# Order of weight conversions and of matmul passes in a fused attention and two-MLP kernel

## The chip, the cores and the metric

The kernel runs on one core of a Trainium2 chip. The metric is the device time of one execution in microseconds (us). Three timed runs of the kernel before gave 647.45, 649.16 and 648.88 us; their median is 648.88 us. A further execution was taken with a profile, and all rows below are from that one.

## The reference

Three stages follow one another, on float32 inputs. The first is a causal linear attention with decay on q, k, v of shape (2, 8, 768, 64); its output, transposed, is x with 1536 tokens of 512 values. The second is a gated MLP, the third an MLP with a cosine:

```python
def _moe_ref(x, w_gate, w_val, w_out):          # 512 -> 1536 -> 512
    g = x @ w_gate
    silu = g * (1.0 / (1.0 + np.exp(-g)))
    val = x @ w_val
    return silu * val @ w_out

def _moe2_ref(x, w_in, w_out):                  # 512 -> 2048 -> 512
    h = x @ w_in
    return (h * np.cos(h)) @ w_out
```

In the reference the weights and inputs have 32 or 64 bits: the inputs are cast to float32, the weights arrive as float64 and are read as pairs of 32-bit words.

## The kernel before, in words

*Number format.* TensorE multiplies tiles of type float32r. To keep precision each operand is split into a high part and a low part (wh and wl, xh and xl, gh and gl), and each product is made of three matmul passes, high by low, low by high and high by high, added in one PSUM bank (`mm3`, L101). One matmul takes a 128x128 stationary operand and a 128x512 moving one. A split (`split`, L96) is a copy on ScalarE, which makes the high part, and then a subtraction on VectorE, or on GpSimd for weights, which makes the low part.

*Conversion of a weight piece.* A piece is 128x512 weights. Its raw words (512 KB) come by a DMA from SyncE's queue into one of three `raw` buffers (`load_piece`, L118). ScalarE makes a scaled copy `ct` (`scale`, L134, two buffers). VectorE builds the float32 value `cw` in three steps (`conv_steps`, L172: L180, L182, L186; three buffers). Then, in the program some operations later, `flush` (L212) writes the split: wh on ScalarE (L98) and wl on GpSimd (L99). When a piece's third step is issued, the next DMA is issued. `convert(t, n)` (L228) runs behind each step of the plan: it issues up to n conversion steps, and more if the next step of the plan needs the piece. A piece has a slot in a ring; 13 slots at first (10 and 3), and 7 more (`RING_C`) when the memory of the x sums is free. `held` (L147) stops a conversion whose slot is still in use. The table `PACE` (L35) gives n by the kinds of operations in a step.

*Stages.* Attention runs in 12 chunks (to about 78 us); the first products of the first MLP run in its last chunks. Tokens lie in three blocks of 512. In the first MLP the first two columns (of 128 of the 1536 inner values) are computed the plain way: per block a gate product of 12 matmuls, a val product of 12, then the activation and a down product of 12 (`op_down`, L631). The other ten columns are seven-product columns, in five groups of two: blocks 0 and 1 and gate and val are treated as a 2x2 by 2x2 product with seven products in place of eight, in four operations q1 (four products, 24 matmuls, L567), q2 (L586), q3 (L596) and q4 (L603) of one product each (6 matmuls). They need sums of weights (sa and sb, four additions on GpSimd, `conv_sums`, L192) and sums of x (t1 to t4, `t_sums`, L518), which are made on VectorE and ScalarE in four stages behind the first plain steps; the scratch space of the sums is the result tile of block 2. Block 2 has plain gate and val products in each group, and down products are put between all these. In the second MLP a step has an in2 product (12 matmuls, `op_in2`, L609) and a down product (12) that belongs to an in2 step three steps earlier; a group has four columns and three blocks, so 12 such steps.

*Activation.* `activation` (L495) multiplies on VectorE (L499), copies gh on ScalarE (L500), and puts gl (L502, VectorE) into a list, `low`, that `low_parts` (L672) empties behind the step's conversions.

*Order.* Each engine executes its instructions in the order in which the program issues them (`manual_schedule`); the loop at L742 to L759 therefore sets the order on every engine. Accumulators and products have four PSUM banks each (`acc` and `mm`). At the end of a group the accumulators are copied (L653, ScalarE, or L655, VectorE, in the first group) or added (L657, VectorE) into the block's sum. At the end of the first MLP the sum y is split on ScalarE and GpSimd (L660), four pieces a block.

Of the kernel before, what the change touches and what calls it, by code (L numbers as in the profile page):

```python
# [20 lines left out]
GROUP1 = 2  # L21
GROUP2 = 4
# [10 lines left out]
RAW_AGE = 2  # L33

PACE = {"gate+val": 2, "gate+val+down": 3, "q1": 4, "down": 1, "gate": 3, "in2": 2, "in2+down": 2}  # L35
WARM = 10
# [4 lines left out]
def kernel(  # L41
# [19 lines left out]
    nc = tc.nc  # L61
# [8 lines left out]
    NF1 = FF1 // P  # L70
# [30 lines left out]
    def mm3(ps, w, x, first, last, **kw):  # L101

        (wh, wl), (xh, xl) = w, x
        nc.tensor.matmul(ps, wh, xl, start=first, stop=False, **kw)  # L104
        nc.tensor.matmul(ps, wl, xh, start=False, stop=False, **kw)  # L105
        nc.tensor.matmul(ps, wh, xh, start=False, stop=last, **kw)  # L106

# [36 lines left out]
    grown = [10 ** 6]  # L144
# [486 lines left out]
    def op_down(ph, blk, f):  # L631
# [10 lines left out]
        for i in range(4):  # L642
            ps = acc[ph, gi, blk][i]
            cs = slice(i * P, (i + 1) * P)
            if ph == 0:
                mm3(ps, (hi[:, cs], lo[:, cs]), (gh, gl), first, last)
            else:
                mm3(ps, (gh[:, cs], gl[:, cs]), (hi, lo), first, last)
            if not last:
                continue  # L650
            sm = sums[ph, blk][:, i, :]
            if first_group and ph == 0:
                nc.scalar.activation(sm, ps, AF.Copy)  # L653
            elif first_group:
                nc.vector.tensor_copy(sm, ps)  # L655
            else:
                nc.vector.tensor_tensor(out=sm, in0=ps, in1=sm, op=ALU.add)  # L657
# [14 lines left out]
    def low_parts():  # L672
        while low:
            low.pop(0)()


    with tc.manual_schedule():
# [62 lines left out]
        begun = len(HALVES) // 2  # L740
        convert(begun - 1, 0)
        for t in range(begun, len(steps)):  # L742
            kinds = [op[0] for op in steps[t]]
            n = PACE.get("+".join(kinds), 0)
            if kinds[0] == "q1":
                if t - begun == 3:
                    t_sums(3)
                convert(t - 1, n)
                n = 0
            for nm, *args in steps[t]:  # L750
                run[nm](*args)
            convert(t, n)
            low_parts()
            if t - begun < 3:
                t_sums(t - begun)
            if steps[t][0] == ("q4", NF1 - 1):
                xt_stack.close()
                ring.append(ctx.enter_context(tc.tile_pool(name="ring_c", bufs=RING_C)))
                grown[0] = n_conv[0]  # L759
# [30 lines left out]
```

## Time and profile before

| | before |
|---|---|
| timed runs, us | 647.45, 648.88 (median), 649.16 |
| profiled execution, us | 646.99 |
| its span, first to last instruction, us | 645.2 |
| TensorE matmul (PE), busy us (share), instructions | 614.3 (95%), 3139 |
| TensorE weight load (PEld) | 500.6 (78%), 3141; one load 0.19 us |
| VectorE (DVE) | 475.0 (74%), 709 |
| ScalarE (ACT) | 295.9 (46%), 506; one gh copy (L500) 0.62 us |
| GpSimd (POOL) | 195.3 (30%), 175; one wl (L99) 1.32 us |
| mean granted TensorE clock | 0.989 |
| DMA | 49.3 MB, 76 GB/s over the span |

The profile is of one execution. A busy time is the sum of an engine's instructions; matmuls overlap, so 614.3 us of PE does not mean that the rest, 31 us, is all that could be saved, and starts of matmuls are a better measure than their busy time. A wait is listed with the instruction that waited, and with the one that released it, as far as semaphores tell. The clock is given as a share of full speed: 1.00 is 2.4 GHz and 0.50 is 1.2 GHz.

### The profile page before, as it was taken

How to read it: one execution, taken by the hardware profiler on the slowest of the kernel's cores; microseconds unless marked ns; L12 is line 12 of the kernel's file. 1: busy time of each engine (PE TensorE's matmuls, PEld its weight loads, DVE VectorE, ACT ScalarE, POOL GpSimd, SP SyncE). 2: the span in 40 equal slices, each digit the busy share in tenths (PEclk: the TensorE clock that was granted, in tenths of full speed). 3: DMA queues.
4: the chain of work that ended last, by engine and by line, in shares of the span. 5: the costliest groups of instructions: out<-in, count | busy, mean ns of one | idle time of the engine just before them, and what ended most of it. 6: DMA issues, size and time to landing. Idle time of an engine off the chain costs nothing.

```text
span 645.2 us, 8290 instructions
## 1 busy us (share of the span) xinstructions
PE 614.3 (95%) x3139; PEld 500.6 (78%) x3141; DVE 475.0 (74%) x709; ACT 295.9 (46%) x506; POOL 195.3 (30%) x175
## 2 busy tenths in 40 slices
PE   8999997898999999999999969999999999999997
PEld 5888885686887887887887857888778877887786
DVE  4677578857787777777777895788688777778655
ACT  2353326544334334434435454555555655555442
POOL 3324305726425425525512751011111111111000
PEclk9999999899999999999999998999999999999999
DMA  9997221121211221222222111211211122220103
GB/s 187 204 238 190 67 66 48 54 93 41 92 56 58 84 66 58 74 65 66 66 66 72 60 36 62 65 56 43 70 61 66 65 66 67 65 66 0 67 1 132
DMA packets 65433, 49.32 MB, mean 76 GB/s; under 512 B 38760, under 2 KB 60272, under 8 KB 65392
## 3 DMA queue, kind: packets, MB, share of 16 engines
q1 hardware_dynamic: 65360, 48.77, 26.7%
q8 instruction: 25, 0.41, 0.3%
q14 instruction: 16, 0.13, 0.1%
q10 hardware_dynamic: 32, 0.01, 0.0%
HBM read 45.61 MB, written 3.15 MB: 76 GB/s over the span
## 4 chain that ended last, share of the span: by engine, by line
PE 69%; DVE 13%; issue 6%; ACT 6%; POOL 4%; DMA 1%; POOLq 0%; DVEq 0%; ACTq 0%
PE acc L104 11%; PE mm L106 10%; PE mm L104 10%; PE mm L105 10%; PE acc L105 10%; PE acc L106 10%; DVE gl L502 2%; ACT gh L500 2%; POOL wl L99 2%; DVE s L499 2%; PE acc L410 2%; PE mm L388 2%; PE acc L416 2%; ACT wh L98 1%; DVE sum L657 1%
## 5 line engine op out<-in xcount | busy, mean ns | idle before, releaser
L99 POOL TENSOR_TENSOR wl<-cw,wh 128x512 fp32r<-128x512 f32 x68 | 89.8, 1322 | 343.6 <-ACT wh L98 325.7
L104 PE MATMUL mm<-xl,wh 128*128 128x512 f32 x376 | 147.0, 391 | 0.0
L105 PE MATMUL mm<-xh,wl 128*128 128x512 f32 x376 | 146.8, 391 | 0.0
L106 PE MATMUL mm<-xh,wh 128*128 128x512 f32 x376 | 146.7, 390 | 0.0
L500 ACT ACTIVATE gh<-s 128x512 fp32r<-128x512 f32 x84 | 52.3, 622 | 91.8 <-DVE s L499 91.8
L502 DVE TENSOR_TENSOR gl<-s,gh 128x512 fp32r<-128x512 f32 x84 | 65.5, 780 | 38.5 <-ACT gh L500 38.0
L104 PE MATMUL acc<-wl,gh 128*128 128x512 f32 x192 | 76.6, 399 | 10.5 <-POOL wl L99 10.5
L104 PEld LDWEIGHTS mm<-xl,wh 128*128 128x128 f32 x376 | 71.1, 189 | 14.9
L105 PEld LDWEIGHTS mm<-xh,wl 128*128 128x128 f32 x376 | 71.0, 189 | 14.9
L106 PEld LDWEIGHTS mm<-xh,wh 128*128 128x128 f32 x376 | 70.9, 189 | 14.8
L105 PE MATMUL acc<-wh,gl 128*128 128x512 f32 x192 | 75.7, 394 | 0.0
L106 PE MATMUL acc<-wh,gh 128*128 128x512 f32 x192 | 75.6, 394 | 0.0
L615 DVE SCALAR_TENSOR_TENSOR s<-s,mm 128x512 f32<-128x512 int32 x48 | 33.0, 686 | 50.2 <-ACT s L614 50.2
L617 ACT ACTIVATE s<-s 128x512 f32<-128x512 f32 x48 | 30.4, 633 | 80.8 <-DVE s L616 80.8
L104 PE MATMUL acc<-gl,wh 128*128 128x512 f32 x144 | 56.8, 394 | 8.2 <-DVE gl L502 6.3
L657 DVE TENSOR_TENSOR sum<-acc,sum 128x512 f32<-128x512 f32 x96 | 60.7, 683 | 2.1 <-PE acc L106 2.1
L105 PE MATMUL acc<-gh,wl 128*128 128x512 f32 x144 | 56.1, 390 | 0.0
L106 PE MATMUL acc<-gh,wh 128*128 128x512 f32 x144 | 56.1, 389 | 0.0
L499 DVE TENSOR_TENSOR s<-s,mm 128x512 f32<-128x512 f32 x71 | 48.3, 680 | 8.8 <-PE mm L106 8.8
L182 DVE SCALAR_TENSOR_TENSOR cw<-ct,cw 128x512 int32<-128x512 int32 x68 | 53.6, 789 | 1.4
L104 PEld LDWEIGHTS acc<-wl,gh 128*128 128x128 f32 x192 | 36.6, 190 | 21.2 <-POOL wl L99 13.8
L186 DVE SCALAR_TENSOR_TENSOR cw<-raw,cw 128x512 int32<-128x512 int32 x68 | 50.7, 745 | 1.3
(125 smaller groups left out, 954.6 us busy)
## 6 DMA issues: line engine op xcount, KB each, us to landing
raw<-in_moe_w_out_dram SPq DMA_DIRECT2D x28, 512.0 KB, 3.3
raw<-in_moe_w_in_dram SPq DMA_DIRECT2D x16, 512.0 KB, 3.7
raw<-in_moe_w_gate_dram SPq DMA_DIRECT2D x12, 512.0 KB, 3.5
raw<-in_moe_w_val_dram SPq DMA_DIRECT2D x12, 512.0 KB, 3.5
q<-in_q_dram SPq DMA_DIRECT2D x12, 256.0 KB, 4.9
k<-in_k_dram SPq DMA_DIRECT2D x12, 256.0 KB, 5.1
v<-in_v_dram SPq DMA_DIRECT2D x12, 256.0 KB, 5.8
out_dram<-sum SPq DMA_DIRECT2D x12, 256.0 KB, 2.0
```

The lines of the kernel that those rows point to most:

```text
L99: (sub or nc.vector).tensor_tensor(out=lo, in0=src, in1=hi.bitcast(F32), op=ALU.subtract)
L104: nc.tensor.matmul(ps, wh, xl, start=first, stop=False, **kw)
L105: nc.tensor.matmul(ps, wl, xh, start=False, stop=False, **kw)
L106: nc.tensor.matmul(ps, wh, xh, start=False, stop=last, **kw)
L182: nc.vector.scalar_tensor_tensor(out=w, in0=t.bitcast(I32), scalar=3, in1=w, op0=ALU.logical_shift_left, op1=ALU.bitwise_or)
L186: nc.vector.scalar_tensor_tensor(out=w, in0=hi, scalar=-0x80000000, in1=w, op0=ALU.bitwise_and, op1=ALU.bitwise_or)
L499: nc.vector.tensor_tensor(out=s, in0=s, in1=up, op=ALU.mult)
L500: nc.scalar.activation(gh, s, AF.Copy)
L502: low.append(lambda: nc.vector.tensor_tensor(out=gl, in0=s, in1=gh.bitcast(F32), op=ALU.subtract))
L615: nc.vector.scalar_tensor_tensor(out=s, in0=n_, scalar=-TWO_PI_1, in1=up, op0=ALU.mult, op1=ALU.add)
L617: nc.scalar.activation(s, s, AF.Abs)
L657: nc.vector.tensor_tensor(out=sm, in0=ps, in1=sm, op=ALU.add)
```

## The change

Five things are done; nothing is computed in another way.

- Ahead of the loop, `convert(begun - 1, 6)` in place of `convert(begun - 1, 0)`: six conversion steps, which are two pieces and the weight sums of the first seven-product unit.
- The number of conversion steps per step of the plan is given by a function, `pace(t)`, in place of the table. In a step with an in2 or down product it is 3 or 2, but 1 where the accumulators are added into the sums; in the other steps it is as before or up to 4 (gate and val with a down), and 2 for gate and val once the ring has grown.
- The order of the three passes: high by high is now second and low by high third in `mm3`; in the first MLP's down product the order is lo by gh, hi by gh, hi by gl, so that gl is used last.
- Low parts of g are not written behind a step if the next step is q4; they then stand behind q4. The fourth stage of the x sums (t4) moves from ahead of the first q1 to behind the down product after the first q2.
- The ring's third part is opened behind the last q3 in place of the last q4. The first group's copies of the second MLP go to ScalarE (L653) in place of VectorE (L655).

```diff
--- before.py
+++ after.py
@@ -31,8 +31,6 @@
 HALVES = (6, 7, 8, 9, 10, 11)
 RAWS = (0, 0, 1, 1, 0, 1, 1, 1, 1, 1, 1, 1)
 RAW_AGE = 2
-
-PACE = {"gate+val": 2, "gate+val+down": 3, "q1": 4, "down": 1, "gate": 3, "in2": 2, "in2+down": 2}
 WARM = 10
 CW = 3
 
@@ -102,8 +100,8 @@
 
         (wh, wl), (xh, xl) = w, x
         nc.tensor.matmul(ps, wh, xl, start=first, stop=False, **kw)
-        nc.tensor.matmul(ps, wl, xh, start=False, stop=False, **kw)
-        nc.tensor.matmul(ps, wh, xh, start=False, stop=last, **kw)
+        nc.tensor.matmul(ps, wh, xh, start=False, stop=False, **kw)
+        nc.tensor.matmul(ps, wl, xh, start=False, stop=last, **kw)
 
 
     up_w = {"gate": w_gate, "val": w_val, "in2": w_in2}
@@ -643,16 +641,16 @@
             ps = acc[ph, gi, blk][i]
             cs = slice(i * P, (i + 1) * P)
             if ph == 0:
-                mm3(ps, (hi[:, cs], lo[:, cs]), (gh, gl), first, last)
+                nc.tensor.matmul(ps, lo[:, cs], gh, start=first, stop=False)
+                nc.tensor.matmul(ps, hi[:, cs], gh, start=False, stop=False)
+                nc.tensor.matmul(ps, hi[:, cs], gl, start=False, stop=last)
             else:
                 mm3(ps, (gh[:, cs], gl[:, cs]), (hi, lo), first, last)
             if not last:
                 continue
             sm = sums[ph, blk][:, i, :]
-            if first_group and ph == 0:
+            if first_group:
                 nc.scalar.activation(sm, ps, AF.Copy)
-            elif first_group:
-                nc.vector.tensor_copy(sm, ps)
             else:
                 nc.vector.tensor_tensor(out=sm, in0=ps, in1=sm, op=ALU.add)
             if last_group and ph == 0:
@@ -738,22 +736,37 @@
         mlp["xt"] = xt_stack.enter_context(tc.tile_pool(name="xt", bufs=1))
         mlp["cs"] = xt_stack.enter_context(tc.tile_pool(name="cs", bufs=2))
         begun = len(HALVES) // 2
-        convert(begun - 1, 0)
+        convert(begun - 1, 6)
+
+        def pace(t):
+
+            kind, last = steps[t][0], steps[t][-1]
+            adds = last[0] == "down" and last[3] % (GROUP1, GROUP2)[last[1]] == (GROUP1, GROUP2)[last[1]] - 1
+            if kind[0] == "q1":
+                return 4
+            if kind[0] in ("gate", "val"):
+                return 4 if last is not kind else 2 if grown[0] < len(pieces) else 3 if kind[0] == "gate" else 0
+            if kind[0] == "down":
+                return 1 if adds else 2
+            if kind[0] == "in2":
+                return 1 if adds else 3
+            return 0
+
         for t in range(begun, len(steps)):
-            kinds = [op[0] for op in steps[t]]
-            n = PACE.get("+".join(kinds), 0)
-            if kinds[0] == "q1":
-                if t - begun == 3:
-                    t_sums(3)
+            n = pace(t)
+            if steps[t][0][0] == "q1":
                 convert(t - 1, n)
                 n = 0
             for nm, *args in steps[t]:
                 run[nm](*args)
             convert(t, n)
-            low_parts()
+            if t + 1 == len(steps) or steps[t + 1][0][0] != "q4":
+                low_parts()
             if t - begun < 3:
                 t_sums(t - begun)
-            if steps[t][0] == ("q4", NF1 - 1):
+            elif t - begun == 6:
+                t_sums(3)
+            if steps[t][0] == ("q3", NF1 - 1):
                 xt_stack.close()
                 ring.append(ctx.enter_context(tc.tile_pool(name="ring_c", bufs=RING_C)))
                 grown[0] = n_conv[0]
```

## Rows read from the trace of the kernel before

**Rows 1.** Waits of TensorE: engine, line, waited for, us in total, times, longest.

```profile
PE acc L104 <- POOL wl L99: 10.5, 8, 5.6
PE acc L104 <- DVE gl L502: 6.3, 4, 2.4
PE mm L104 <- ACT wh L98: 3.1, 1, 3.1
PE mm L105 <- POOL wl L99: 2.4, 1, 2.4
PE acc L104 <- ACT sum L653: 1.8, 1, 1.8
```

**Rows 2.** Timeline of TensorE: start us, duration us, engine, line, operation, [wait].

```profile
89.77 0.39 PE L104 MATMUL mm<-xl,wh 128*128 128x512 f32 x1
...
95.21 0.39 PE L104 MATMUL acc<-gl,wh 128*128 128x512 f32 x1
```

**Rows 3.** Timeline of TensorE, first down product of block 2.

```profile
126.91 0.50 PE L104 MATMUL acc<-gl,wh 128*128 128x512 f32 x1 [1.81 <-ACT sum L653]
```

**Rows 4.** Windows: stretch, us, busy PE, PEld, DVE, ACT, POOL, clock, DMA, GB/s.

```profile
112.50:119.00 6.50, 5.36 (x13) 4.20 (x14) 6.46 (x4) 2.29 (x4) 3.73 (x3) 0.50 0.18 68
385.50:392.00 6.50, 4.86 (x11) 3.80 (x12) 4.16 (x7) 3.70 (x7) 2.55 (x2) 0.50 0.28 81
...
450.00:520.00 70.00, 68.55 (x301) 56.12 (x300) 55.19 (x90) 38.85 (x65) 10.32 (x8) 1.00 0.20 62
```

**Rows 5.** Timeline of TensorE: the same down product in two column groups.

```profile
206.01 0.50 PE L104 MATMUL acc<-gl,wh 128*128 128x512 f32 x1 [1.30 <-DVE gl L502]
...
253.88 0.50 PE L104 MATMUL acc<-gl,wh 128*128 128x512 f32 x1 [1.29 <-DVE gl L502]
```

**Rows 6.** Timeline of TensorE: waits of down products in the second MLP.

```profile
387.14 0.80 PE L104 MATMUL acc<-wl,gh 128*128 128x512 f32 x1 [5.59 <-POOL wl L99]
...
456.77 0.50 PE L104 MATMUL acc<-wl,gh 128*128 128x512 f32 x1 [0.92 <-POOL wl L99]
...
524.09 0.50 PE L104 MATMUL acc<-wl,gh 128*128 128x512 f32 x1 [0.92 <-POOL wl L99]
```

**Rows 7.** Timeline of GpSimd: splits and weight sums of the first unit.

```profile
111.88 3.92 POOL L99 TENSOR_TENSOR wl<-cs,wh 128x512 fp32r<-128x512 f32 x2
...
122.27 0.79 POOL L203 TENSOR_TENSOR cs<-cw 128x256 f32<-128x256 f32 x1 [1.88 <-DVE cw L186]
...
125.66 1.27 POOL L99 TENSOR_TENSOR wl<-cw,wh 128x512 fp32r<-128x512 f32 x1
```

**Rows 8.** Timeline of VectorE, 87 to 118 us.

```profile
87.32 0.69 DVE L499 TENSOR_TENSOR s<-s,mm 128x512 f32<-128x512 f32 x1 [2.10 <-PE mm L106]
87.93 0.42 DVE L180 TENSOR_SCALAR cw<-raw 128x512 int32<-128x512 int32 x1
...
89.72 0.69 DVE L502 TENSOR_TENSOR gl<-s,gh 128x512 fp32r<-128x512 f32 x1
90.32 1.22 DVE L538 TENSOR_TENSOR sum<-xh,xl 128x1024 f32<-128x1024 f32 x1
...
96.37 0.68 DVE L499 TENSOR_TENSOR s<-s,mm 128x512 f32<-128x512 f32 x1
...
110.69 1.78 DVE L502 TENSOR_TENSOR gl<-s,gh 128x512 fp32r<-128x512 f32 x1
112.39 2.28 DVE L552 TENSOR_TENSOR sum<-xh,sum 128x1024 f32<-128x1024 f32 x1
...
116.81 1.21 DVE L532 TENSOR_TENSOR t2l<-sum,t2h 128x1024 fp32r<-128x1024 f32 x1
```

**Rows 9.** Timeline of ScalarE: the four accumulator copies behind a down product.

```profile
97.63 2.04 ACT L653 ACTIVATE sum<-acc 128x512 f32<-128x512 f32 x4
```

**Rows 10.** DMA issues: timeline of SyncE; the page's last part (us to landing).

```profile
85.29 0.37 SPq L125 DMA_DIRECT2D raw<-in_moe_w_gate_dram  x1
...
raw<-in_moe_w_gate_dram SPq DMA_DIRECT2D x12, 512.0 KB, 3.5
```

## The prediction, made before the change was run

> **What bounds the kernel now.** I read four views in this order: the waits of TensorE, its timeline at each of them, the windows of those stretches, and the timelines of VectorE (DVE), ScalarE (ACT) and GpSimd (POOL) ahead of the waits. The reader is to see that TensorE is the bound and that it is held up in few places. After the attention part it issues one 128x512 matmul every 0.2267 us at full clock (24 of them between the two starts of [rows 2]), whatever the operands. Its waits are five groups [rows 1]: for weights' low parts from POOL (10.5 us in 8 waits, and 2.4), for a high part from ACT (3.1), for the low part of g from DVE (6.3 in 4), for an accumulator's release by ACT (1.8). Placed in time they make four losses:
>
> A, the first seven-product unit. From the start at 95.21 [rows 2] to the down product of block 2 at 126.91 [rows 3] lie 90 matmuls (12 down, 24 up and 12 down, 24 of q1, 12 down, 6 of q2), 20.4 us at 0.2267; it took 31.7. Lost: 11.3, part of it at 1.2 GHz (granted clock 0.50 from 112.5 to 119 [rows 4], after the waits for wh and wl).
>
> B, the five column groups. A group has 204 matmuls, 46.25 us; from 206.01 to 253.88 it took 47.87 [rows 5], so 1.6 are lost at a down product that waits 1.3 for gl. The first group waits 1.1 longer (6.3 less three times 1.3 is 2.4), the fifth only about 0.3: 3 x 1.6 + 2.6 + 0.3 = 7.7.
>
> C, the entry into the second MLP: 5.6 us for wl at 387.14 [rows 6], then 1.2 GHz until about 392 (granted 0.50 [rows 4]), which costs half of 5.0: 8.1.
>
> D, the steady second MLP: 288 matmuls are 65.3 us, the period is 67.3 (456.77 to 524.09 [rows 6]), so 2.0 in three groups and 0.7 in the first: 6.8.
>
> **The change part by part.** Matmuls, DMAs and conversions are the same in number; all is order; DMAs that start sooner find the engines 0.2 busy [rows 4]. The sum is made against the profiled execution, 646.99 us (span 645.2); the median of the runs shown, 648.88, is 1.9 above it.
>
> *Conversions per step and the ring (C, D).* In the code before, the four out2 pieces of a group are split when only the 12 matmuls of the in2 product (2.7 us) stand between the split and its use; the last DVE step, ACT's wh, POOL's wl (1.27 [rows 7]) don't fit into that. With three DVE steps in each in2 step without sums (nine of twelve) and one with them, 30 can run per group against 24 needed. Following the convert loop through the code, the first four out2 pieces are then issued 84 to 108 matmuls ahead (19 us or more), later ones 130 and more; the ring's seven slots come two steps sooner, just before they are wanted. 19 us also cover the POOL queue at the entry (twelve yl splits). Cost of the denser steps: DVE is busy 55.19 of 70 us in the second MLP [rows 4], 4.3 of each 5.44 us step; the third conversion step adds about 0.6 (three took 1.79 from 87.93 to 89.72 [rows 8]), so 4.9, still hidden under TensorE; without that cover each step would lose the excess. ACT, at 38.85 of 70, takes the twelve first-group copies from DVE (0.5 each [rows 9]); behind each stands only the next unit's quotient, due 2.7 us later. I take all of D, 6.8, and of C 8.1: no wait, so no clock drop either. Bounds: nothing gained, or all 14.9.
>
> *Low part of g in the third pass, deferred low parts (B).* In the down product of the first MLP the first pass now uses lo and gh, the third gl. Before, gl of val stands between val's and q4's work on DVE; deferring it brings q4's gh forward past one gl, which beside a POOL split took 1.78 in place of 0.69 [rows 8]. The down starts 2.7 us (12 matmuls of gate) after q4 ends; the chain to gh is a product of 0.7 and ACT's 0.6, so gh is in time, and gl, behind two gl's on DVE, has 0.45 us more. Left: up to 0.3 per group where POOL splits run beside. I take 7.0 of 7.7; bounds 3 and 7.7. The second MLP's downs lose nothing by the exchange: wl of their first pass is the one that C and D made early. The up products need xl first as before. Where two passes in a row now have the same stationary operand, no row shows what a repeated load costs; all loads (0.19 each by the profile's table) lie beside matmuls 0.2267 apart, so I take nothing, and bound it by nothing gained and, were it not hidden, 0.19 on each repeat, which no row suggests.
>
> *Six conversion steps ahead of the first unit (A).* This is where I expect no gain. The weights are no longer late, but the sums of x (t1 to t4) stand on the same DVE queue behind the added conversions, and what is late next is t2l. Step by step, with the rows' times:
> 1. Two pieces of three steps (1.8 each) and a wait of 0.4 for ACT's scaled copy now come after the step whose end lets the DMA of 85.29 start [rows 10], so to 89.8. Then ACT's scaled copy of a third piece waits for that DMA, which lands 3.5 later, at 88.8; queued behind it is the Silu of the gate, and for that the product L499. That product moves from 87.32 to 90.05: 2.7.
> 2. The next conversion's L180 writes the third-last cw buffer, which POOL reads: its four sum additions take 3.4 (122.27 to 125.66 [rows 7]) after 89.8, a split 1.3, so 94.4. DVE would be there at 92.5: 1.9, plus 0.45 for the step.
> 3. The five sums of stage 0 (1.22 alone) now run beside three POOL splits. Beside such splits a sum took 2.28, and two splits 3.92 in place of 2.6 [rows 8, 7]. Five us at about half speed: 2.3, between 0 and 4.
> So the product of 96.37 [rows 8] stands at 96.4 + 2.7 + 2.35 + 2.3 = 103.7. Behind it on ACT are gh and the four accumulator copies [rows 9], so the down of block 1, due at 103.4, waits first.
> 4. From that product to the end of t2l it was 21.65 us (96.37 to 118.02 [rows 8]). Two more conversion steps (1.2), one more scaled copy before t1h (0.55) and more splits beside the sums (about 0.5) make 23.9: t2l at 127.6. q2 needs it. TensorE would be there at 114.3 (84 matmuls after 95.21); two waits on the same DVE queue, for t1l and for the bank that val's product frees, bring it to about 121 by the same additions, still before t2l.
> 5. Behind t2l on DVE stand three conversion steps (1.9) and q1's sum (0.7), then on ACT the Silu and a wh (0.6 each) and the accumulator copy (0.5): the down of block 2 starts at 131.9 in place of 126.9. That is 5.0 lost. t4, moved behind q2's down, lies there beside that down and q3.
> Bounds: all of 11.3 gained, if DVE overlaps what I put in a row; 7 lost, if the POOL splits block the sums outright. I take 5.0 lost, since it is built from rows of this very stretch.
>
> The Trainium skill's page "SBUF — State Buffer", section "Who interferes with whom", says that a DVE instruction with two SBUF inputs and a GpSimd instruction that reads SBUF exclude each other for the whole instruction, so that the loser stops altogether. The rows of point 3 show both slowed, neither stopped throughout. By the rule the three splits would hold up the sums by their full 3.9, which alone makes the time 1.6 longer than mine, near 632.5.
>
> *Sum.* 646.99 + 5.0 - 7.0 - 8.1 - 6.8 = 630.1. The timed runs shown lie 0.5 to 2.2 above the profiled execution; with 1 for that I predict 631.
>
> **The rivals.**
> *The first unit gains as well* (20%). For it: the waits there name weights alone [rows 1], 5.5 us of them, and DVE sat idle about 2 us before 87.32. Against it: DVE is busy nearly all of 112.5 to 119 [rows 4] while TensorE waits. If three quarters of A go, 8.5: 647 - 8.5 - 21.9 = 616.6, with 1 added 618; a half way result, A unchanged, is 626.
> *The column groups or the entry keep their waits* (13%). The denser conversions put more POOL splits beside gl and gh; a gl there took 1.78 [rows 8]. If B gives 2 and C half, 9 less is gained: 640.
> *The conversion steps make DVE the bound of the second MLP* (the other side, 4%). A step of 24 matmuls has 5.44 us. From 4.9 it would take two DVE instructions per step that lose 0.5 to 1 us beside a POOL split. DVE decides from 5.44 on; at 5.9 per step in some 36 steps the 16.9 gained are given back, and at 6.1 it is 24 us, 655. Against it: in 450 to 520 POOL is busy only 10.3 of 70, and the whole work to be converted is the same.
> That the order of passes or the ring does nothing is covered by the second.
>
> **How the numbers follow.** Forecast 63%: 625 to 634 by itself. First unit gaining: 614 to 624. Waits kept: 634 to 642. DVE bound: 640 to 655, half of it slower. For 8 in 10 I take 619 to 638. A measurement of this kernel can tell about 0.3% (2 us) from no change. Faster by more: 0.95; within: 0.02; slower: 0.03.
>
> **What would show it.** Right: no wait for wl in the second MLP and a period of 65.3; full clock from 380 to 390; column groups of 46.3 to 46.6; in the first unit waits of TensorE for t1l, for an accumulator copy and for t2l, with the down of block 2 near 132 and DVE without idle from 90 to 127. Wrong: that down before 122 (then DVE was not the bound there and the time falls under 625), or downs of the second MLP that wait for gh or gl.

## The result, and the profile after

The changed kernel takes 640.53 us (median; 639.93 to 640.76 in 4 runs) against 648.16 for the kernel before (the median of its three timed runs and the profiled one): a ratio of 0.9881, 95% interval 0.9861 to 0.9902. That is 7.6 us faster; 631 was predicted, with a range of 619 to 638. The sign was right, the size was not. The profiled execution took 640.58 us, its span is 638.8.

Line numbers of the changed kernel are those of before less two in most places: L97 is wl, L102 to L104 the three passes, L644 to L646 those of the first MLP's down product, L178, L180 and L184 the conversion steps, L497, L498 and L500 the activation, L536 to L540 the first sums of x, L530 their low parts, L580 and L598 the sums of q1 and q3, L614 and L615 steps of the cosine, L653 the copies of accumulators on ACT, L655 their sums on DVE.

The waits of TensorE after the change (engine, line, waited for, us in total, times, longest):

```profile
PE mm L102 <- DVE s L580: 8.1, 1, 8.1
PE acc L644 <- ACT sum L653: 4.4, 1, 4.4
PE acc L102 <- ACT sum L653: 2.2, 1, 2.2
PE mm L102 <- DVE s L497: 2.2, 1, 2.2
PE acc L102 <- DVE sum L655: 1.3, 1, 1.3
```

Against [rows 1], every wait for gl and for a weight is gone, and in their place stands DVE: one wait of 8.1 us for an addition. Placed on the timeline (start, duration, operation, [wait]):

```profile
108.28 0.80 PE L644 MATMUL acc<-gh,wl 128*128 128x512 f32 x1 [4.36 <-ACT sum L653]
115.00 0.50 PE L102 MATMUL mm<-t1l,wh 128*128 128x512 f32 x1 [0.86 <-DVE t1l L530]
120.21 0.50 PE L102 MATMUL mm<-xl,wh 128*128 128x512 f32 x1 [2.19 <-DVE s L497]
134.30 0.80 PE L102 MATMUL mm<-t2l,wh 128*128 128x512 f32 x1 [8.10 <-DVE s L580]
137.03 0.63 PE L644 MATMUL acc<-gh,wl 128*128 128x512 f32 x1
...
212.71 0.39 PE L644 MATMUL acc<-gh,wl 128*128 128x512 f32 x1
258.96 0.39 PE L644 MATMUL acc<-gh,wl 128*128 128x512 f32 x1
...
380.48 0.47 PE L102 MATMUL acc<-wl,gh 128*128 128x512 f32 x1 [1.34 <-DVE sum L655]
404.73 0.60 PE L102 MATMUL acc<-wl,gh 128*128 128x512 f32 x1 [2.21 <-ACT sum L653]
441.13 0.39 PE L102 MATMUL acc<-wl,gh 128*128 128x512 f32 x1
506.41 0.39 PE L102 MATMUL acc<-wl,gh 128*128 128x512 f32 x1
```

The first five starts are the first seven-product unit: q2 starts at 134.30, the down product of block 2 at 137.03 and not at 126.91 [rows 3]. Next stands the same down product of two column groups, 46.25 us apart where it was 47.87 [rows 5]. The last four are the second MLP: two waits at its entry that weren't there before, and then the same down product one group later, 65.28 us and no wait, where it was 67.3 [rows 6]. The windows (columns as in [rows 4]) show the clock behind the waits at 134.30 and 404.73, and the steady second MLP:

```profile
134.00:140.00 6.00, 5.70 (x16) 4.52 (x17) 2.65 (x5) 4.31 (x8) 1.28 (x1) 0.60 0.30 87
404.50:409.00 4.50, 4.27 (x12) 3.40 (x13) 2.21 (x4) 3.02 (x7) 1.27 (x1) 0.62 0.00 0
450.00:520.00 70.00, 70.00 (x310) 57.99 (x309) 60.09 (x96) 44.21 (x77) 15.47 (x11) 1.00 0.24 76
```

The first two stretches are partly at 1.2 GHz (a mean granted clock of 0.60 and 0.62). In the third DVE is busy 60.09 of 70 us, 4.9 more than in [rows 4], 4.7 per step of 5.44: about the 4.9 predicted, and hidden.

To compare kernels, one measure is used from here on: for each start of a TensorE matmul that comes over 0.25 us behind the start before it, the excess over 0.2265, the interval at full clock, is added up; waits and half clock both count. A is the first seven-product unit (90 to 143 us), B the column groups (to 362), C the entry of the second MLP (to 420), D the rest. The sums are of the profiled execution, the times are medians, and each ratio is to the kernel before on the same chip, whose median lay between 647.1 and 648.2 us; where two kernels ran on different chips, the ratios compare them better than the times.

| kernel | A | B | C | D | sum | time, us | ratio to before [95%] |
|---|---|---|---|---|---|---|---|
| before | 11.4 | 7.9 | 9.0 | 6.0 | 34.3 | 648.16 | |
| after | 21.7 | 0.1 | 5.8 | 0 | 27.6 | 640.53 | 0.9881 [0.9861, 0.9902] |
| before + ahead part | 20.7 | 6.7 | 9.3 | 6.0 | 42.7 | 655.42 | 1.0116 [1.0096, 1.0137] |
| before + order of passes | 11.3 | 5.6 | 8.3 | 6.0 | 31.2 | 645.32 | 0.9961 [0.9945, 0.9977] |
| before + paces and ring | 17.4 | 6.7 | 2.9 | 0 | 27.0 | 639.35 | 0.9878 [0.9861, 0.9896] |
| after, no ahead part | 14.4 | 0.2 | 5.7 | 0 | 20.3 | 630.95 | 0.9747 [0.9723, 0.9771] |
| after, first q1 bare | 19.5 | 0.2 | 5.6 | 0 | 25.3 | 637.10 | 0.9836 [0.9804, 0.9868] |
| after, copies on DVE | 21.3 | 0.2 | 2.9 | 0 | 24.4 | 637.61 | 0.9844 [0.9823, 0.9865] |
| after, sums first | 10.8 | 1.0 | 5.6 | 0 | 17.4 | 630.25 | 0.9730 [0.9711, 0.9749] |
| sums first, splits twice (one run) | 12.1 | 1.4 | 4.1 | 0 | 17.5 | 630.31 | |
| both mended | 8.4 | 2.1 | 2.9 | 0 | 13.4 | 626.52 | 0.9673 [0.9649, 0.9697] |
| both mended, thin entry | 8.8 | 2.1 | 0 | 0 | 10.9 | 623.44 | 0.9631 [0.9618, 0.9644] |

The sums explain the times: before to after 6.7 of the 7.6 us. B gains 7.8, C 3.2 and D 6.0, and A gives 10.3 of these 17.0 back.

### The profile page after: what moved, and what is told of

Read it like the earlier page. It is cut to its first block, busy times and chain, and to the rows that moved or that the text cites. A ratio compares the mean times of both kernels' runs of the same rounds, so it can differ in the third digit from the quotient of the medians.

```text
span 638.8 us, 8317 instructions
## 1 busy us (share of the span) xinstructions
PE 612.7 (96%) x3139; PEld 502.4 (79%) x3141; DVE 465.3 (73%) x697; ACT 302.2 (47%) x518; POOL 198.0 (31%) x175
## 4 chain that ended last, share of the span: by engine, by line
PE 79%; DVE 13%; ACT 3%; issue 3%; DMA 2%; POOL 1%; DVEq 0%; POOLq 0%; ACTq 0%
PE mm L102 13%; PE mm L103 13%; PE mm L104 13%; PE acc L102 7%; PE acc L103 7%; PE acc L104 7%; PE acc L644 4%; PE acc L645 4%; PE acc L646 4%; DVE cw L180 2%; DVE gl L500 2%; PE acc L408 2%; PE mm L386 2%; PE acc L414 2%; PE mm L329 1%
## 5 line engine op out<-in xcount | busy, mean ns | idle before, releaser
L97 POOL TENSOR_TENSOR wl<-cw,wh 128x512 fp32r<-128x512 f32 x68 | 94.5, 1394 | 272.3 <-ACT wh L96 235.8
L102 PE MATMUL mm<-xl,wh 128*128 128x512 f32 x376 | 146.6, 390 | 2.2 <-DVE s L497 2.2
L104 PE MATMUL mm<-xh,wl 128*128 128x512 f32 x376 | 146.4, 389 | 0.0
L498 ACT ACTIVATE gh<-s 128x512 fp32r<-128x512 f32 x84 | 52.3, 623 | 84.7 <-DVE s L497 84.7
L500 DVE TENSOR_TENSOR gl<-s,gh 128x512 fp32r<-128x512 f32 x84 | 64.3, 769 | 36.1 <-ACT gh L498 36.0
L102 PEld LDWEIGHTS mm<-xl,wh 128*128 128x128 f32 x376 | 70.6, 188 | 17.6 <-DVE s L497 2.6
L104 PEld LDWEIGHTS mm<-xh,wl 128*128 128x128 f32 x376 | 70.6, 188 | 14.6
L102 PE MATMUL acc<-wl,gh 128*128 128x512 f32 x192 | 75.5, 393 | 3.6 <-ACT sum L653 2.2
L104 PE MATMUL acc<-wh,gl 128*128 128x512 f32 x192 | 75.4, 392 | 0.0
L615 ACT ACTIVATE s<-s 128x512 f32<-128x512 f32 x48 | 30.4, 633 | 80.0 <-DVE s L614 80.0
L644 PE MATMUL acc<-gh,wl 128*128 128x512 f32 x144 | 58.1, 403 | 4.4 <-ACT sum L653 4.4
L655 DVE TENSOR_TENSOR sum<-acc,sum 128x512 f32<-128x512 f32 x96 | 59.7, 681 | 2.1 <-PE acc L104 2.1
L180 DVE SCALAR_TENSOR_TENSOR cw<-ct,cw 128x512 int32<-128x512 int32 x68 | 55.9, 822 | 4.5 <-ACT ct L139 3.0
L645 PE MATMUL acc<-gh,wh 128*128 128x512 f32 x144 | 57.5, 399 | 0.0
L646 PE MATMUL acc<-gl,wh 128*128 128x512 f32 x144 | 57.3, 398 | 0.0
L184 DVE SCALAR_TENSOR_TENSOR cw<-raw,cw 128x512 int32<-128x512 int32 x68 | 55.1, 810 | 1.4
L497 DVE TENSOR_TENSOR s<-s,mm 128x512 f32<-128x512 f32 x71 | 48.3, 681 | 8.5 <-PE mm L104 8.5
L96 ACT ACTIVATE wh<-cw 128x512 fp32r<-128x512 f32 x68 | 41.7, 621 | 17.7 <-DVE cw L184 17.7
```

The source lines that it names most:

```text
L97: (sub or nc.vector).tensor_tensor(out=lo, in0=src, in1=hi.bitcast(F32), op=ALU.subtract)
L104: nc.tensor.matmul(ps, wl, xh, start=False, stop=last, **kw)
L180: nc.vector.scalar_tensor_tensor(out=w, in0=t.bitcast(I32), scalar=3, in1=w, op0=ALU.logical_shift_left, op1=ALU.bitwise_or)
L184: nc.vector.scalar_tensor_tensor(out=w, in0=hi, scalar=-0x80000000, in1=w, op0=ALU.bitwise_and, op1=ALU.bitwise_or)
L498: nc.scalar.activation(gh, s, AF.Copy)
L500: low.append(lambda: nc.vector.tensor_tensor(out=gl, in0=s, in1=gh.bitcast(F32), op=ALU.subtract))
```

## The experiments

**The first unit.** The rows of DVE's and then POOL's timeline after the change, from which the theory was made:

```profile
90.71 0.68 DVE L497 TENSOR_TENSOR s<-s,mm 128x512 f32<-128x512 f32 x1
...
96.14 1.50 DVE L178 TENSOR_SCALAR cw<-raw 128x512 int32<-128x512 int32 x1 [1.89 <-POOL wl L97]
97.56 1.77 DVE L500 TENSOR_TENSOR gl<-s,gh 128x512 fp32r<-128x512 f32 x1
99.26 2.31 DVE L536 TENSOR_TENSOR sum<-xh,xl 128x1024 f32<-128x1024 f32 x1
101.60 1.23 DVE L537 TENSOR_TENSOR sum<-sum,xh 128x1024 f32<-128x1024 f32 x1
...
106.40 0.68 DVE L497 TENSOR_TENSOR s<-s,mm 128x512 f32<-128x512 f32 x1
...
110.79 1.33 DVE L180 SCALAR_TENSOR_TENSOR cw<-ct,cw 128x512 int32<-128x512 int32 x1 [2.05 <-ACT ct L139]
...
129.57 2.28 DVE L530 TENSOR_TENSOR t2l<-sum,t2h 128x1024 fp32r<-128x1024 f32 x1
131.77 0.41 DVE L178 TENSOR_SCALAR cw<-raw 128x512 int32<-128x512 int32 x1
...
133.56 0.68 DVE L580 TENSOR_TENSOR s<-mm,s 128x512 f32<-128x512 f32 x1
```

```profile
94.81 2.54 POOL L97 TENSOR_TENSOR wl<-cw,wh 128x512 fp32r<-128x512 f32 x2
97.32 3.17 POOL L97 TENSOR_TENSOR wl<-cs,wh 128x512 fp32r<-128x512 f32 x2
```

From 90 us to the end of t2l DVE stands idle for 1.89 before 96.14 and for 2.05 before 110.79, where it waits for ACT's scaled copy, and for little else. While POOL's four splits run (94.81 to 100.5), a conversion step L178 takes 1.50 (0.42 alone, at 131.77), a gl 1.77 (0.69 alone), a sum 2.31 (1.23 alone, in the next row). And t2l ends at 131.85, but q2 starts at 134.30: three conversion steps and L580 are between.

*The ahead part alone, in the kernel before.*

```diff
-        convert(begun - 1, 0)
+        convert(begun - 1, 6)
```

> The kernel before with one part of the change: six conversion steps ahead of the loop, all else as before. Theory Q (the first unit is set by the number of DVE instructions ahead of t2l and of q1's sum, which q2 needs because it adds to the bank that this sum reads): conversion steps ahead of t2l go from 27 to 33, ahead of q1's sum from 31 to 37, against 36 and 39 in the changed kernel; q2 starts near 130 to 132 instead of 123.4, and the time is 6 to 8 us longer than before, about 655. Rival W (the late weights were the loss, and what the changed kernel lost there comes from its other parts): the waits for wh and wl go, q2 starts near 118, time 641 to 643.

Measured: 655.42 us (654.46 to 655.6). This one edit costs 7.4 us (the kernel before took 647.97 on the same chip). The start of q2:

```profile
132.18 0.79 PE L104 MATMUL mm<-t2l,wh 128*128 128x512 f32 x1 [8.44 <-DVE s L582]
```

It takes the place of a wait of 0.39 at 123.44 in the kernel before, and the down of block 2 starts at 134.91, 8.0 later than [rows 3]. The theory that the ahead part makes the loss in the first unit holds; that it helps and something else hurts is out.

*The change without the ahead part.*

```diff
-        convert(begun - 1, 6)
+        convert(begun - 1, 0)
```

> The changed kernel with no conversion steps ahead of the loop (that one part undone). Conversion steps ahead of t2l 30 in place of 36, ahead of q1's sum 34 in place of 39; the weights of the first unit are late again as in the kernel before. Theory Q: the loss of the first unit falls from 21.6 us to 13 or 14, time 631 to 634, so the part that was meant to help costs 7 to 9 us within the whole change. Rival W (with the other parts in place the weights would be late and cost as much): the waits for wh and wl return with half clock, 639 to 642.

Measured: 630.95 us (630.69 to 632.71), 9.6 less than the whole change, or 8.7 by the ratios; the profiled execution is the one of 632.71, and its sum is 7.3 less. The waits for weights come back beside a smaller one for L580:

```profile
PE mm L102 <- ACT wh L96: 4.6, 1, 4.6
PE mm L102 <- DVE s L580: 3.8, 1, 3.8
PE mm L104 <- POOL wl L97: 1.6, 1, 1.6
```

Weights that come 4.6 and 1.6 us late cost less than sums that come 8.1 late. A still lost 14.4, against 11.4 before.

*The first q1's conversions behind q1.* In the change they stand ahead of q1, and so ahead of its sum L580 on DVE.

```diff
-                convert(t - 1, n)
-                n = 0
+                convert(t - 1, n if t - begun > 3 else 0)
+                n = 0 if t - begun > 3 else n
```

> The changed kernel with the conversion steps that stand ahead of the first q1 (three on DVE, between t2l and q1's sum) issued behind q1. Theory Q: q1's sum comes 1.9 to 2.4 us sooner, q2 starts near 132 instead of 134.3, time 637.5 to 639 against 640.5. Rival P (TensorE waits there for the splits on POOL and the copies on ACT, whose order is unchanged): less than 0.5 us.

Measured: 637.10 us (635.70 to 638.97), 3.4 less, or 2.9 by the ratios. q2 starts 2.4 sooner, just behind L580; 0.6 of that is attention, which ended sooner in this execution, and the rest is what three conversion steps take:

```profile
131.92 0.80 PE L102 MATMUL mm<-t2l,wh 128*128 128x512 f32 x1 [7.91 <-DVE s L580]
```

A falls by 2.2; the rest of the 3.4 is within what the runs of this kernel spread. That q2 hangs on L580 is plain in the code: q2 adds into the bank (`ps["a"]`) that L580 reads.

*Sums first.* The six conversion steps ahead stay, but no others come before the x sums: none in the three plain steps, the first q1's behind q1, three per step in the unit's down steps.

```diff
+            if t - begun < 3:
+                return 0
+            if t - begun < 10 and kind[0] == "down":
+                return 3
...
+                convert(t - 1, n if t - begun > 3 else 0)
+                n = 0 if t - begun > 3 else n
```

> The changed kernel with no optional conversion step in the three plain steps ahead of the first unit nor ahead of its q1, and three in each down step of that unit instead; the six steps ahead of the loop stay. Conversion steps ahead of t2l 24, ahead of q1's sum 24, against 36 and 39. Theory Q: 12 steps of 0.6 to 1 us less ahead of t2l, 15 less ahead of the sum: q2 starts between 117 and 122 instead of 134.3, time 626 to 630. Rival P (POOL's splits beside the sums and the DMA that ACT waits for set it): the four splits and the waiting copy are still there; q2 near 130, time 636 to 638.

Measured: 630.25 us (629.9 to 630.45).

```profile
117.84 0.50 PE L102 MATMUL mm<-t2l,wh 128*128 128x512 f32 x1 [1.10 <-DVE s L580]
131.00 0.79 PE L102 MATMUL mm<-xl,wh 128*128 128x512 f32 x1 [4.20 <-DVE s L598]
```

DVE does 8 conversion steps from 78 us to t2l where the change has 20, and q2 is 16.5 us sooner (0.5 of it by attention). So the ahead part itself can stay; what hurts is the number of steps in front of t2l and L580. Whether it helps there the runs don't show: sums first without it was not run. But 4.2 us come back at 131.00: q4 waits for L598 behind the conversions that were pushed there.

*POOL's four splits of the unit's weights written twice, in the kernel with sums first.* This asks what splits on POOL cost DVE by themselves.

```diff
             split(wh, wl, fp[key], sub=nc.gpsimd)
+            if key in (("gate", 2), ("val", 2), ("sa", 2), ("sb", 2)):
+                nc.gpsimd.tensor_tensor(out=wl, in0=fp[key], in1=wh.bitcast(F32), op=ALU.subtract)
```

> The kernel with the sums first (no optional conversions ahead of the first unit), in which POOL writes the four low parts of the first unit's weights twice; the DVE queue is unchanged. Theory C (a DVE instruction with two operands in SBUF that meets a split on POOL takes about 1.1 us longer): four more splits meet four or more of the sums, val's product that frees the bank and t2l come 4 to 5 us later, q2 starts near 122 instead of 117.8, time about 634. Rival N (the long sums do not come from POOL): t2l and the time as without, 630, within 0.5.

Measured: one run, 630.31 us: no later than with the splits once, but the places of the loss changed. DVE with the splits twice, and then the same three instructions with the splits once (line numbers differ by two):

```profile
104.05 1.63 DVE L502 TENSOR_TENSOR gl<-s,gh 128x512 fp32r<-128x512 f32 x1 [0.69 <-ACT gh L500]
106.94 2.22 DVE L532 TENSOR_TENSOR t1l<-sum,t1h 128x1024 fp32r<-128x1024 f32 x1 [1.26 <-ACT t1h L529]
109.09 2.31 DVE L532 TENSOR_TENSOR t3l<-sum,t3h 128x1024 fp32r<-128x1024 f32 x1
```

```profile
103.89 0.69 DVE L500 TENSOR_TENSOR gl<-s,gh 128x512 fp32r<-128x512 f32 x1 [0.70 <-ACT gh L498]
106.79 1.23 DVE L530 TENSOR_TENSOR t1l<-sum,t1h 128x1024 fp32r<-128x1024 f32 x1 [2.21 <-ACT t1h L527]
107.93 1.22 DVE L530 TENSOR_TENSOR t3l<-sum,t3h 128x1024 fp32r<-128x1024 f32 x1
```

Each instruction that meets a split takes 0.9 to 1.1 us more, the small one and the large ones alike. t2l ends at 119.44 and not 117.19, and the wait for val's bank at 114.57 is 2.33 us where it was 0.83. In the table A rises by 1.3 and B by 0.4. The time did not follow because C falls by 1.5: in the entry the wait of 2.2 us was not followed by half clock in this run. So contention is shown on the instructions; t2l came later by half of the expected 4 to 5 us, and the time, of a single run, shows nothing of it.

**The entry of the second MLP.**

*The first group's copies back on DVE.*

```diff
-            if first_group:
+            if first_group and ph == 0:
                 nc.scalar.activation(sm, ps, AF.Copy)
+            elif first_group:
+                nc.vector.tensor_copy(sm, ps)
```

> The changed kernel with the first group's accumulator copies of the second MLP back on DVE; all else unchanged. Theory S (the wait of 2.2 us and the half clock behind it at 404.7 come from the place of the copies on ACT behind gh): the wait and the clock drop go, time 636.5 to 637.5 against 640.5. Rival L (DVE and ACT are late there by some 3 us after POOL's twelve yl splits, and any engine would bring the copies late): the copy comes about 0.8 sooner on DVE, 1 to 1.5 us of wait stays, time 639 to 640.

Measured: 637.61 us (636.69 to 638.42), 2.9 less, or 2.4 by the ratios; C falls by 2.9.

```profile
379.33 0.47 PE L102 MATMUL acc<-wl,gh 128*128 128x512 f32 x1 [1.30 <-DVE sum L657]
402.45 0.47 PE L102 MATMUL acc<-wl,gh 128*128 128x512 f32 x1 [1.10 <-DVE sum L655]
```

The wait for the copies, 2.21 at 404.73 in the change with half clock behind it, is now 1.10 at full clock. ACT's timeline in the change shows why it was longer there:

```profile
402.29 0.63 ACT L615 ACTIVATE s<-s 128x512 f32<-128x512 f32 x1 [1.48 <-DVE s L614]
...
403.58 0.61 ACT L498 ACTIVATE gh<-s 128x512 fp32r<-128x512 f32 x1
404.10 0.57 ACT L653 ACTIVATE sum<-acc 128x512 f32<-128x512 f32 x1
```

ACT comes to the copies only behind the two cosine steps and a gh of its queue, and the first of these waited 1.48 for DVE's L614. So the size of the gain is that of the one theory, and the wait that stays is that of the other: moving the copies to ACT was a loss of 2.4 to 2.9, but they are late on either engine.

*Both places mended:* sums first (with six conversion steps in the first down step of the unit, none in the next, and none at the first q1) and the copies on DVE.

```diff
+            if t - begun < 3:
+                return 0
+            if t - begun < 10 and kind[0] == "down":
+                return {4: 6, 6: 0}.get(t - begun, 3)
...
-                convert(t - 1, n)
+                convert(t - 1, n if t - begun > 3 else 0)
                 n = 0
```

> The kernel with the sums first, with six conversion steps in the down step behind the first q1, none behind the first q2 and three behind the other downs of that unit, so that the conversion no longer stands ahead of q3's sum and waits for a buffer; and with the copies of the second MLP's first group on DVE. Theory Q: the wait of 4.2 us for q3's sum and the half clock behind it go (6 of the 6.5 us there), and the copies give the 3 us that they gave alone: 621 to 623 against 630.25. Rival: the wait moves to q4 or to the weights of the second unit, and 3 us alone are gained: 627.

Measured: 626.52 us (626.41 to 626.61), at full clock in the profiled execution (a mean of 1.000). The rival was nearer than the 621 to 623 of the theory: the waits are smaller, but they moved. A falls by 2.4 and C by 2.7, but B rises from 1.0 to 2.1, because a down product now waits 1.61 for gl at 155.44.

```profile
130.14 0.50 PE L102 MATMUL mm<-xl,wh 128*128 128x512 f32 x1 [2.27 <-DVE s L598]
369.10 0.47 PE L102 MATMUL acc<-wl,gh 128*128 128x512 f32 x1 [1.30 <-DVE sum L657]
392.23 0.47 PE L102 MATMUL acc<-wl,gh 128*128 128x512 f32 x1 [1.12 <-DVE sum L655]
```

*Fewer conversions at the entry, on top.*

```diff
-                return 1 if adds else 3
+                return 1 if adds or kind[1] < 2 and kind[2] < GROUP2 else 3
```

> Built on the kernel with both places mended (626.5 us), which still waits 1.30 at 369.10 for the accumulators' adds L657 and 1.12 at 392.23 for the first copies L655, 2.75 in all with the pipeline's refill. Here the in2 steps of blocks 0 and 1 in the first group of the second MLP run one conversion step, not three. Theory L (the entry is late because a step's own chain there, DVE L613 and L614, then six ACT instructions of which wh and the scaled copy belong to conversions, takes 4.95 of the 5.44 us of a step, and so the lag from the end of the first MLP is worked off by only 0.5 us a step): without two thirds of the conversions it is worked off before 392, the wait there goes and that at 369 goes or shrinks under 0.5; 623.5 to 624.8 us. Rival P (the lag is POOL's twelve yl splits and ACT's yh beside the adds, whatever is converted): both waits stay within 0.4 of their size, 626 to 627 us. Should a weight be late (its lead falls from 84 to 36 matmuls, 8 us), a wait for wl shows after 395.

Measured: 623.44 us (623.27 to 624.0); beside it on the same chip the mended kernel with the late ring (below) took 625.43. Both entry waits are gone. Windows of 366 to 395, first the mended kernel, then this one:

```profile
366.00:395.00 29.00, 26.58 (x116) 21.41 (x116) 27.37 (x39) 18.19 (x32) 12.12 (x8) 1.00 0.23 73
```

```profile
366.00:395.00 29.00, 29.00 (x130) 24.01 (x129) 24.52 (x36) 17.80 (x32) 8.12 (x6) 1.00 0.12 37
```

TensorE goes from 26.58 of 29 us to all 29.00. POOL is busy 8.12 us and not 12.12, DVE 24.52 and not 27.37. The theory that the entry is late by the conversions in it holds, and the rival, that POOL's yl splits and ACT's yh alone make it late, falls. Whether it is ACT's scaled copy and wh in the chain from L614 to the next quotient, or DVE's own steps, the run doesn't tell apart: both went together.

*The ring opened late again, in the mended kernel.*

```diff
-            if steps[t][0] == ("q3", NF1 - 1):
+            if steps[t][0] == ("q4", NF1 - 1):
```

> The kernel with both places mended (626.5 us), but the ring's third part is opened behind the last q4, as before the change. Theory: the opening behind q3 is worth nothing, since out2 pieces are issued 84 and more matmuls (19 us) ahead either way and the shortest lead falls to 36 matmuls (8 us), more than ACT's and POOL's split take: 626.1 to 627.0 us, no wait for wl in the second MLP. Rival: the two steps sooner matter, a wait for wl of 0.5 to 2 us comes back near 369 to 395: 627.3 to 629 us.

Measured: 625.43 us (625.18 to 625.69), ratio 0.9660 [0.9647, 0.9674], where the mended kernel had 0.9673 [0.9649, 0.9697]. Not slower: in this kernel the earlier opening is worth nothing that the runs can tell. The entry waits only shift, 0.27 and 1.45 for 1.30 and 1.12.

*t4's high part sooner, on the thin entry:* ACT's copy behind the first down step, DVE's low part where it was.

```diff
-        else:
+        elif stage == 3:
             high(4, t24)
+        else:
             lows(4, t24)
...
-            elif t - begun == 6:
-                t_sums(3)
+            elif t - begun in (4, 6):
+                t_sums((t - begun + 2) // 2)
```

> As the kernel with the thin entry, and the high part of t4 (ACT L527) is written two steps sooner, behind the first down step after the first q1, its low part (DVE L530) stays where it was. Theory: the wait of 2.27 at 130.14 is L598 queued on DVE behind that low part, which waits 3.73 for the high part queued on ACT behind four wh; with the high part there sooner the low part runs at about 124.2 and L598 right after q3, the wait goes and nothing else in the unit is late before gl at 155: 2.0 to 2.6 less than the thin entry alone. Rival: DVE is the bound of the unit, the wait moves to gh or gl of q3 or q4 behind it, under 1 us is gained.

Measured: 623.47 us (622.29 to 623.76), where the thin entry alone took 623.44: no gain in the median. The wait of 2.26 for L598 is gone as expected, that sum (L599 in this kernel) now runs at 125.05 and q4 starts at 127.23 without a wait. But 14 matmuls on:

```profile
132.97 0.73 PE L104 MATMUL mm<-xh,wl 128*128 128x512 f32 x1 [2.41 <-POOL wl L97]
```

This is the second column's q1, which waits for the low part of its weight sum: POOL's additions began only at 122.50, behind the conversions that were put behind the sums of x. The size is that of the rival, but the wait went to neither gh nor gl: the weights are late again, by DVE's conversions and POOL's work behind them.

**Parts of the change alone.**

*The order of passes alone, in the kernel before* (`mm3` and the first MLP's down product as in the change, gl not deferred).

```diff
-        nc.tensor.matmul(ps, wl, xh, start=False, stop=False, **kw)
-        nc.tensor.matmul(ps, wh, xh, start=False, stop=last, **kw)
+        nc.tensor.matmul(ps, wh, xh, start=False, stop=False, **kw)
+        nc.tensor.matmul(ps, wl, xh, start=False, stop=last, **kw)
...
-                mm3(ps, (hi[:, cs], lo[:, cs]), (gh, gl), first, last)
+                nc.tensor.matmul(ps, lo[:, cs], gh, start=first, stop=False)
+                nc.tensor.matmul(ps, hi[:, cs], gh, start=False, stop=False)
+                nc.tensor.matmul(ps, hi[:, cs], gl, start=False, stop=last)
```

> The kernel before with the order of the passes alone changed, nothing deferred and no conversion moved. Theory O (two edits share what the column groups gained: the third pass gives 0.45, the deferral brings gh forward): a wait of 0.5 to 0.8 us for gh or gl stays in each group, time 3 to 4 us shorter than before, 644 to 645. Rival A (the order alone is enough): all waits of the column groups go, 640 to 641.

Measured: 645.32 us (643.67 to 646.15), 2.5 less by the ratio, where 3 to 4 were expected. The waits for gl (6.3 in 4) became waits for gh (3.7 in 4): 0.66 in three groups, as expected, and 1.74 in the first. B fell from 7.9 to 5.6 and to 0.1 in the whole change, which also defers gl; so the order alone is less than a third of B's gain.

*The paces and the ring alone, in the kernel before* (function `pace` of the change, ring behind q3).

> The kernel before with the new paces of conversion and the ring opened sooner, nothing else. Theory (the parts add): all waits for wl in the second MLP go (6.8 of D and the 5.6 with its clock drop, 8.1), the two new waits of 2.6 together come in at the entry as where the copies stayed on DVE, and gl's waits (6.3) stay: first unit as in the change without the conversions ahead, so 635 to 637 us. Rival (the parts need one another: the denser conversions put POOL's splits beside gl and make its waits longer, or out2's pieces are late without the other order of passes): 638.5 us or more, with gl's waits over 7.5 in all or a wait for wl after 380.

Measured: 639.35 us (638.40 to 641.02), later than the 635 to 637 expected, though not by the rival's means: gl's waits are 5.3 in all, no weight is late in the second MLP, C is the 2.9 of the kernels with copies on DVE. What is more is A, 17.4:

```profile
PE acc L104 <- DVE gl L502: 5.3, 5, 1.1
PE mm L104 <- ACT wh L98: 4.6, 1, 4.6
PE mm L104 <- DVE s L582: 4.6, 1, 4.6
```

The denser paces put 14 conversion steps ahead of t2l and not 11, t2l starts at 119.09 and not 116.81, and q2 at 128.84 and not 123.44. So the paces cost 6.0 in the first unit even without the ahead part; in the change without the ahead part, which has the same 14 steps but moves t4 behind q2 and changes the order of passes, it is 3.0.

## Why the prediction was wrong, point by point

The forecast missed by 9.5 us: A is 5.3 and C 4.9 worse than taken, B 0.8 better and D 0.8 worse (10.2 together; the sums explain 0.9 less of the gain than the times do).

*B: right.* Predicted 7.0 of 7.7 gained; 7.9 became 0.1. The order of passes alone gives 2.3 of it. The waits that it leaves are for gh, which the prediction said the deferral would bring forward; that the deferral gives the rest is not shown, since no run has it without the other parts.

*D: right.* Predicted 6.8; no wait is left behind 409, and the period is 65.28.

*C: wrong.* The step that failed is "I take all of D, 6.8, and of C 8.1: no wait, so no clock drop either", and in it the twelve copies on ACT, "behind each stands only the next unit's quotient". The waits for wl did go. But of 8.1 only 3.2 was gained, because two new waits came (1.34 for DVE's last adds at 380.48, 2.21 for the copies at 404.73) and 1.2 GHz behind the second. For a moved copy the question was what stands ahead of it in its queue, not behind: ahead of them stood the cosine and a gh that DVE's lag had made late. 5.8 us are lost in C, where 9.0 were before. With the copies on DVE 2.9 is left, and with one conversion step in place of three in the in2 steps of blocks 0 and 1 none. DVE's load per step was forecast right (4.7 against 4.9) for the steady part; the entry isn't steady, since there the adds of the last sums, yh, yl and the copies come on top.

*A: the sign right, the size half.* Predicted 5.0 lost, with 7 as the worst bound; measured 10.3. Of these 7.3 go with the ahead part (21.7 to 14.4 without it) and 3.0 with the rest of the change. The steps, each against the timeline above (attention ended 0.4 later in this execution, which is taken off):
1. The first product at 90.05: 90.3. Right.
2. The wait for the cw buffer to 94.4: 95.7. POOL's four additions started 0.7 later than taken and lasted 3.9 and not 3.4. Off by 1.3.
3. Contention at stage 0: 2.3 predicted; three instructions lost 1.08 each, 3.2. With steps 1 and 2 the second product came at 106.0 and not 103.7.
4. From there to the end of t2l: 23.9 predicted, 25.45 measured. Off by 1.5.
5. From t2l to the down of block 2: 4.3 predicted, 5.2 measured. The three conversion steps and L580 were counted, but as ahead of q1's Silu alone. That path was wrong: they stand ahead of q2 as well, since q2 adds into the bank that L580 reads: TensorE stood for 8.1 us in one piece, and the six matmuls of q2 then took 2.7 at half clock, so that the down didn't wait for the copy on ACT, which the prediction had as the last link. Some 0.7 more were lost behind it at half clock.

Steps 2 to 4 mostly have one cause, the term that was mis-sized: the price of an added conversion step. Between 78 us and t2l DVE does 20 conversion steps and not 11; that count was right (six, one and two more were costed). They take 16.6 us and not 6.8, so 1.09 for each added one, where the prediction took 0.6, the price of a step with nothing beside it: 9.8 us and not 5.4. The prediction had the price of company in its own rows (a sum of 2.28, a gl of 1.78 [rows 8]) and charged it to the sums, 2.3 and 0.5, and to no conversion step. Of its signs, DVE was not without idle (1.89 and 2.05), and TensorE waited for L580 and not for t2l.

The Trainium skill's page "SBUF — State Buffer", section "Who interferes with whom", gives an exclusive lock between GpSimd and those DVE instructions that have two SBUF inputs, and says that a tensor_scalar can take part in it. By that rule step 3 would have cost 3.9 where 2.3 was taken; 3.2 was measured, so the rule was nearer, and L178, a tensor_scalar on a single tensor, was indeed held up as much as the sums.

*The rivals.* The first unit gaining as well fell; that its waits "name weights alone" also passed over the 1.81 for an accumulator copy in [rows 3]. DVE as the bound of the second MLP fell for the steady part. The rival at 640 gave the time that came out, but by other means: it had the column groups keep their waits, and these went; only its half of the entry came true, and the rest of the 9 us is A. The 8-in-10 range failed by A and C together: 5.3 or 4.9 alone would have ended near 636, inside it. That the time came out at the rival's 640 is chance.

## What to carry to other kernels

When work is moved ahead on a queue that is busy anyway, name first what else is due on that queue and price the moved work by what its neighbours make of it, not by its time alone: here weights that were 5.5 us late in two waits were exchanged for a sum that was 8.1 us late. For each moved instruction look at what stands ahead of it, and at what else waits for what stands behind it: here q2 adds into the bank that L580 reads, so everything put ahead of L580 also held up q2. Give a new pace to the steady part of a loop, and keep it off the seams, where copies, adds and splits come together.

The best kernel of these runs (with t4's high part sooner it is no faster that the runs can tell) keeps the order of passes, the deferral, the paces and the six steps ahead of the loop, puts the unit's other conversions behind the sums of x, copies on DVE and thins the entry: 623.44 us, 0.9631 [0.9618, 0.9644], where the change alone has 0.9881.

## What the runs showed of the hardware

- A DVE instruction that lay wholly in a run of POOL's splits took 0.9 to 1.1 us more whatever its size: 0.42 to 1.50, 0.69 to 1.77, 1.23 to 2.31 (a split alone takes 1.3). Those at the edge of a run took less more, as the 1.33 at 110.79 for 0.69.
- The same wait of 2.2 us at the entry was followed by 1.2 GHz, with matmul starts 0.40 to 0.43 us apart for some 3.7 us, in the change and with sums first, and by none with the splits written twice (2.21 at 396.04), which is worth some 1.7 us. Likewise the wait for L598 in the unit: 2.27 with both mended at full clock, 2.26 with the thin entry and 1.2 GHz behind it. What tells the cases apart the runs don't show.
